# Storing each 128-row output tile by two 64-row transfers instead of one with an outer dimension of two

## The chip, the core and the metric

The kernel runs on one core of a Trainium2 chip. The metric is the time in microseconds (us) that one execution takes on the device, as the median of several runs. The engines are PE (TensorE, matrix products; PEld is its loading of weights), DVE (VectorE), ACT (ScalarE), POOL (GpSimd) and SP (SyncE). In this kernel SP issues every transfer between HBM and on-chip memory, one after the other; 16 DMA engines move the bytes.

## What is computed

A linear attention with a decaying state, over 4 batches, 8 heads, 768 tokens and head size 48, followed by a feed-forward layer whose activation is the square of a relu:

```python
for t in range(S):                       # state: [B, H, D, D]
    cur = einsum('bhd,bhe->bhde', u * k[t], v[t])
    y[t] = einsum('bhd,bhde->bhe', r[t], state + cur)
    state = w[t][..., None] * state + einsum('bhd,bhe->bhde', k[t], v[t])
x = y as [3072 tokens, 384]
out = square(maximum(x @ w_in, 0)) @ w_out        # w_in 384x2048, w_out 2048x384
```

Inputs and output are float32; the matrix products run in bfloat16.

## The kernel before, in words

The 3072 tokens are cut into 12 steps of 256 tokens, three steps for each batch. Within a step a partition holds two neighbouring tokens, an even and an odd one (`j` = 0 or 1), so that a 256-token block of `r`, `k`, `v` or `w` is one load of 384 KB into a tile of 128 partitions (`load_step`, L93). Four buffers of each input are there.

Attention of a step goes roughly so: `ww_` (POOL, L177) multiplies neighbouring decays, `lw_` (ACT, L181) takes the logarithm, `cum_` (PE, L217 to L220) sums it, `exp_` (ACT, L225 and L227) takes the exponential, `rd_` (DVE, L234) scales `r` and `k`. The result is transposed to `rkT`: by PE (L245) and a copy (L254) in the first four steps, by a transposing transfer from SP (`dtr_`, L257) in the other eight. `p_` (PE, L270) and `pm_` (DVE, L276) make the scores inside a block; `su_`, `ts_` and `sn_` (PE L290, DVE L299 and L301, POOL L305) carry the state on; `y_` and `yb_` (PE, L315) sum up the output. ACT casts `v` (`v_`, L185) for this, and POOL makes the terms of the current token (`ku_`, `qp_`, `vq_`, L197, L202 and L210). `y` is cast (L357) and transposed to `xT`, by PE in the first four steps and by a transposing transfer (`dyt_`, L373) in the others.

The feed-forward layer of a step then has 48 matmuls into the wide layer (`m1_`, L386), relu and square on ACT or DVE (L393, L395, L401, L403), and 32 matmuls back (`m2_`, L410), 16 for each of two tiles of 128 tokens (`c` = 0 or 1). `os_` (ACT, L415) copies such a tile from the accumulator to `o_sb`, 128 partitions by 384 float32, and `store` (L419) writes it out. There are 24 of these tiles, and four buffers for them.

In `o_sb`, partitions 0 to 63 hold the even tokens of the tile and partitions 64 to 127 the odd ones, while in the output even and odd rows alternate. The one transfer of `store` therefore has a three-dimensional target: 2 (even, odd) by 64 rows by 384 numbers, with the dimension of two outermost.

The order of all instructions is fixed when the kernel is built. A planner (`make_order`) knows for every operation (`op`) its engine, an assumed cost, a rank and what it depends on; for a transfer it also knows how long SP takes to issue it and how long the transfer is taken to occupy the DMA engines. It plays the schedule through and writes each engine's instructions in the order that comes out. On the chip each engine then works through its own list in that order and waits where an operand isn't there yet. So a wait holds up everything behind it on its engine, and a changed cost in the planner can change the order on every engine. The transfers use eight completion semaphores in turn, so each also waits until the one eight before it has landed.

Of the kernel before, what the change touches and what calls it, by code (L numbers as in the profile page):

```python
# [18 lines left out]
def kernel(  # L19
# [13 lines left out]
    nc = tc.nc  # L33
    PSUM = bass.MemoryType.PSUM

    B, H, S, D = r.shape
    C = 128
    Q = 64
# [101 lines left out]
    for c in range(2):  # L140
        rows = slice(c * Q, (c + 1) * Q)
# [21 lines left out]
    for c in range(2):  # L163
        rows = slice(c * Q, (c + 1) * Q)
# [7 lines left out]
    tiles = {}  # L172
# [243 lines left out]

    def store(s, c):
        t0 = s * T + c * C
        nc.sync.dma_start(out=out[t0:t0 + C, :].rearrange("(p j) d -> j p d", j=2),  # L419
                          in_=tiles.pop(("o", s, c))[:])  # L420

    def warm_(n):
        ps = ps_m2.tile([C, 512], FP32, name="m2")
# [9 lines left out]
    def op(eng, us, rank, fn, args, deps, take=(), give=None, dma=None):  # L433
        key = (fn.__name__,) + args
        plan[key] = (eng, us, rank, fn, args, deps, take, give, dma)

    def on(name, s, *rest):
        return [(name, s) + rest] if s >= 0 else []

    def by_dma(s):  # L440
        return s >= DMA_FROM
# [58 lines left out]
    for s in range(NS):  # L500
        at = AHEAD + s * 200
        xt = ("dyt_", s) if by_dma(s) else ("xt_", s)
        for g in range(8):
            deps = [xt] + [("cast", "i", g // 2, j) for j in range(KT)]
            if s >= 3:
                deps.append(("m2_", s - 3, 1, 3))
            op("P", .66, at + g, m1_, (s, g), deps, take=("m1",) if g % 2 else ("m1", "rl"))
            op(dict(A=.60, V=.68), None, at, rl_, (s, g), [("m1_", s, g)], give="m1")
            if g % 2:
                op(dict(A=1.05, V=.75), None, at, sq_, (s, g // 2), [("rl_", s, g - 1), ("rl_", s, g)],  # L510
                   give="rl")
        for c in range(2):
            for q in range(4):
                deps = [("sq_", s, q)]
                deps += [("cast", "o", q, j) for j in range(4)]
                if q:
                    deps.append(("m2_", s, c, q - 1))
                op("P", .65, at + AFTER + c * 4 + q, m2_, (s, c, q), deps,
                   take=() if q else ("m2",))
            op("A", .50, at - 5000, os_, (s, c), [("m2_", s, c, 3)] + on("store", s - 2, c), give="m2")  # L520
            op("S", .36, -1, store, (s, c), [("os_", s, c)], dma=(8, .54, 1.0))

    seq = [(0, x) for x in "wrukv"] + [(1, x) for x in "wrkv"] + [(g, "i") for g in range(4)]
    seq += [(2, x) for x in "wrkv"] + [(g, "o") for g in range(4)]
# [6 lines left out]
    for n, x in seq:  # L531
# [12 lines left out]
        dma = {"i": (24, 2.05, .9), "o": (32, 2.1, .9), "u": (8, .6, .9)}.get(x, (64, 1.73, .9))  # L544
# [147 lines left out]
```

## Time and profile before

| what | value |
|---|---|
| median of three runs | 230.69 us (230.67 to 230.79) |
| the profiled execution | 231.1 us |
| its span in the profile | 229.3 us |
| PE busy | 195.4 us, 85% of the span |
| DVE, ACT, POOL busy | 133.3, 109.0, 109.9 us |
| granted TensorE clock, mean | 0.967 |
| DMA traffic | 36.23 MB, mean 158 GB/s |
| stores of output tiles | 24, of 192 KB each, 0.52 us to issue (median) |

The profile is of one execution; all times "at" some point are us from the start of its span. The span leaves out 1.8 us that the device's own time of the same execution has (231.1 less 229.3). The views used below are the engines' busy time in stretches of time, which ends with the granted clock (1.00 is full speed), the mean busy share of the 16 DMA engines and the GB/s that they moved; the chain of work that ended last, which shows for each moment what the end of the run was waiting for; the instructions in order of time; and the list of who waited for whom. A sequencer's issue of a transfer is written SPq.

### The profile page before, as it was taken

Reading aid. Unit: us, or ns where it says so; the run is one execution under the profiler, and the core shown is the slowest. Engines: PE = TensorE matmul, PEld = TensorE weight load, DVE = VectorE, ACT = ScalarE, POOL = GpSimd, SP = SyncE. Lnnn points to the kernel's source line nnn. Section 1 sums busy time; section 2 is a strip of 40 time slices with the busy share of each in tenths; the row PEclk is TensorE's granted clock in tenths of the full one; section 3 lists DMA queues with packets and bytes.
Section 4 is the critical chain, followed back from the end, with each engine's and each line's share of the span. In section 5 each row is a group of like instructions: output and inputs, shape, how many; then the busy total and the mean of one; then the engine's idle time right before and its main releaser. Section 6 shows DMA issues by size and latency. Waiting matters only on the chain.

```text
span 229.3 us, 6128 instructions
## 1 busy us (share of the span) xinstructions
PE 195.4 (85%) x2637; PEld 130.3 (57%) x2637; DVE 133.3 (58%) x191; ACT 109.0 (48%) x177; POOL 109.9 (48%) x108
## 2 busy tenths in 40 slices
PE   7779999999989598897599994969498899999840
PEld 2335776667657354565366572747275577777520
DVE  4676897868759337283197754846376546445300
ACT  3418968876742466283573653460561332222200
POOL 6399595499983855931947733563720000000000
PEclk9999999999999979999799999999799999999995
DMA  7999999996697689946969659689948216111111
GB/s 170 236 300 377 262 304 362 223 273 174 176 121 209 164 81 238 150 125 168 204 162 219 152 155 138 172 139 177 118 81 104 51 33 65 38 39 38 37 50 38
DMA packets 80218, 36.23 MB, mean 158 GB/s; under 512 B 73408, under 2 KB 78656, under 8 KB 80192
## 3 DMA queue, kind: packets, MB, share of 16 engines
q1 hardware_dynamic: 80192, 35.86, 72.2%
q8 instruction: 20, 0.33, 0.6%
q14 instruction: 6, 0.05, 0.1%
HBM read 25.36 MB, written 4.72 MB: 131 GB/s over the span
## 4 chain that ended last, share of the span: by engine, by line
DMA 36%; PE 33%; SPq 9%; POOL 7%; ACT 4%; issue 4%; DVE 2%; POOLq 0%
PE m L410 14%; PE m L386 14%; DMA v_raw<-in_v_dram 10%; DMA w_raw<-in_w_dram 8%; SPq L93 6%; DMA w_st<-in_moe_w_in_dram 5%; DMA w_st<-in_moe_w_out_dram 4%; DMA k_raw<-in_k_dram 3%; DMA rkT<-rdec_buf 3%; DMA xT<-y_sb 3%; PE att L315 3%; POOL vq L210 2%; POOL ww L177 2%; POOL r_raw L189 1%; SPq L103 1%
## 5 line engine op out<-in xcount | busy, mean ns | idle before, releaser
L386 PE MATMUL m<-xT,wi_sb 128*128 128x256 bf16 x576 | 79.0, 278 | 4.1 <-ACT rl L393 2.6
L410 PE MATMUL m<-wo_sb,gt 128*128 128x384 bf16 x384 | 77.4, 331 | 5.4 <-ACT o_sb L415 5.0
L386 PEld LDWEIGHTS <-wi_sb 128*128 128x128 bf16 x576 | 55.6, 100 | 20.7 <-issue 5.4
L395 DVE TENSOR_SCALAR rl<-m 128x512 f16<-128x512 f32 x50 | 34.3, 690 | 34.7 <-PE m L386 34.7
L410 PEld LDWEIGHTS <-gt 128*128 128x128 bf16 x384 | 35.9, 98 | 25.9 <-issue 8.3
L393 ACT ACTIVATE rl<-m 128x512 f16<-128x512 f32 x46 | 27.1, 594 | 37.8 <-PE m L386 37.5
L276 DVE TENSOR_TENSOR pmT<-att,mask 128x1024 bf16<-128x1024 f32 x24 | 28.6, 1219 | 9.2 <-PE att L270 8.2
L401 ACT ACTIVATE gt<-rl 128x1024 bf16<-128x1024 f16 x24 | 25.3, 1056 | 1.3 <-DVE rl L395 0.7
L197 POOL TENSOR_TENSOR ku<-k_raw,u_bc 128x768 f32<-128x768 f32 x12 | 22.9, 1910 | 5.1 <-DMA k_raw<-in_k_dram 5.1
L210 POOL TENSOR_TENSOR vq<-v_raw,q 128x768 bf16<-128x768 f32 x12 | 17.9, 1491 | 14.0 <-DMA v_raw<-in_v_dram 4.5
L177 POOL TENSOR_TENSOR ww<-w_raw 128x384 f32<-128x384 f32 x11 | 11.0, 1000 | 25.1 <-DMA w_raw<-in_w_dram 25.1
L202 POOL TENSOR_TENSOR ku<-ku,r_raw 128x768 f32<-128x768 f32 x12 | 21.7, 1810 | 0.7
L185 ACT CAST v_bf<-v_raw 128x768 bf16<-128x768 f32 x12 | 10.0, 831 | 24.9 <-DMA v_raw<-in_v_dram 24.9
L415 ACT ACTIVATE o_sb<-m 128x384 f32<-128x384 f32 x24 | 11.7, 487 | 19.0 <-PE m L410 18.7
L403 DVE TENSOR_TENSOR gt<-rl 128x1024 bf16<-128x1024 f16 x24 | 18.1, 752 | 3.1 <-ACT rl L393 1.6
L425 PE MATMUL m<-warm 128*128 128x512 bf16 x61 | 18.0, 425 | 1.2 <-DVE half_ones L145 1.2
L193 POOL TENSOR_TENSOR k_raw<-k_raw,w_raw 128x384 f32<-128x384 f32 x11 | 11.7, 1062 | 8.6 <-DMA k_raw<-in_k_dram 8.1
L270 PE MATMUL att<-rkT 64*64 64x128 bf16 x384 | 8.9, 222 | 6.5 <-DMA rkT<-rdec_buf 6.4
L206 DVE TENSOR_REDUCE q<-ku 128x16 f32<-128x768 f32 x12 | 11.3, 944 | 5.1 <-POOL ku L202 5.1
L305 POOL TENSOR_TENSOR S<-t_state,a_c 128x192 bf16<-128x192 f32 x20 | 11.4, 571 | 6.0 <-DVE t_state L301 5.8
L301 DVE TENSOR_TENSOR t_state<-S,att 128x192 f32<-128x192 bf16 x16 | 5.6, 351 | 14.7 <-POOL S L305 11.7
L181 ACT ACTIVATE lw_buf<-ww 128x384 bf16<-128x384 f32 x12 | 6.2, 517 | 15.0 <-POOL ww L177 11.8
(64 smaller groups left out, 177.8 us busy)
## 6 DMA issues: line engine op xcount, KB each, us to landing
w_raw<-in_w_dram SPq DMA_DIRECT2D x12, 384.0 KB
r_raw<-in_r_dram SPq DMA_DIRECT2D x12, 384.0 KB
k_raw<-in_k_dram SPq DMA_DIRECT2D x12, 384.0 KB
v_raw<-in_v_dram SPq DMA_DIRECT2D x12, 384.0 KB
out_dram<-o_sb SPq DMA_DIRECT2D x24, 192.0 KB
w_st<-in_moe_w_in_dram SPq DMA_DIRECT2D x4, 768.0 KB
w_st<-in_moe_w_out_dram SPq DMA_DIRECT2D x4, 768.0 KB
rkT<-rdec_buf SPq DMA_TRANSPOSE x16
```

Of the source, the lines that this page charges most:

```text
L177: mul(ww[:], raw["w", s][:, :, 0, :], raw["w", s][:, :, 1, :])
L197: nc.gpsimd.tensor_mul(ku[:], raw["k", s][:, :, 1:3, :], u_bc[:, :, None, :].to_broadcast([C, H, 2, D]))
L202: nc.gpsimd.tensor_mul(ku[:], ku[:], raw["r", s][:, :, 0:2, :])
L210: nc.gpsimd.tensor_mul(vq[:].rearrange("p j h d -> p h j d"), raw["v", s][:], tiles.pop(("q", s))[:, :, :, None].to_broadcast([C, H, 2, D]))
L276: nc.vector.tensor_mul(tiles["pmT", s][:, f].rearrange("p a j t -> p a (j t)"), tiles.pop(("p", s, f))[:].rearrange("p e (a x) -> p (e a) ...
L386: nc.tensor.matmul(ps1[:, j, :], wi_sb[:, kk, n * 128:(n + 1) * 128], tiles["xT", s][:, :, kk, :], start=(kk == 0), stop=(kk == KT - 1))
L393: nc.scalar.activation(rl, m1[:], AF.Relu, scale=RS)
L395: nc.vector.tensor_scalar(out=rl, in0=m1[:], scalar1=RS, scalar2=0.0, op0=ALU.mult, op1=ALU.max)
L401: nc.scalar.activation(gt, rl[:], AF.Square)
L403: nc.vector.tensor_mul(gt, rl[:], rl[:])
L410: nc.tensor.matmul(tiles["m2"][:], gt[:, n, c * C:(c + 1) * C], wo_sb[:, n, :], start=(n == 0), stop=(n == NT - 1))
L425: nc.tensor.matmul(ps[:], warm[:, 0:C], warm[:], start=True, stop=True)
```

## The change

Each tile is stored by two transfers of 64 rows: the even tokens from partitions 0 to 63 and the odd tokens from partitions 64 to 127. Both sides of each are 64 rows by 384 numbers. The planner's figures for a store go with it: SP's issue from 0.36 to 0.9 us for the pair, and the time on the DMA engines from 0.54 to 0.6 us.

```diff
     def store(s, c):
         t0 = s * T + c * C
-        nc.sync.dma_start(out=out[t0:t0 + C, :].rearrange("(p j) d -> j p d", j=2),
-                          in_=tiles.pop(("o", s, c))[:])
+        o_sb = tiles.pop(("o", s, c))
+        rows = out[t0:t0 + C, :].rearrange("(p j) d -> j p d", j=2)
+        for j in range(2):
+            nc.sync.dma_start(out=rows[j], in_=o_sb[j * Q:(j + 1) * Q, :])
...
-            op("S", .36, -1, store, (s, c), [("os_", s, c)], dma=(8, .54, 1.0))
+            op("S", .9, -1, store, (s, c), [("os_", s, c)], dma=(8, .6, 1.0))
```

Because the planner's figures change, the order of later instructions changes too, on every engine. In the built program SP issues 129 transfers instead of 105; the lists of the engines agree up to the first steps and then differ in places: `rl` and `gt` pieces move between ACT and DVE (two instructions fewer on DVE, one more on ACT), and on SP one `k_raw` load near the end stands ahead of a transpose and a store that it stood behind.

## The prediction

> **What bounds the kernel now.** I read the busy time by stretches first. PE is the engine with the most work, so the question is where it stands idle:
>
> ```profile
> 72.00:180.00 108.00, 89.09 (x1330) 60.10 (x1327) 60.68 (x78) 52.11 (x83) 56.48 (x48) 0.95 0.83 151
> 180.00:217.00 37.00, 36.84 (x345) 26.58 (x344) 19.59 (x28) 11.88 (x21) 0.00 (x0) 1.00 0.20 41
> ```
>
> The columns are the stretch, its length, busy us of PE, PEld, DVE, ACT and POOL, granted clock, DMA share and GB/s. From 180 to 217 us PE has no idle time to give back. From 72 to 180 us it is idle for 108.0 - 89.1 = 18.9 us. The clock of 0.95 there is three dips: stretches of 3.4 us from 81.0, 111.7 and 162.9 show a clock of 0.50, each after a PE gap of 2 to 4 us. Half speed for 3 x 3.4 us loses 5.1 us. So 24.0 us stand in this stretch, and then there is the end, 217 to 229 us.
>
> Next the chain that ended last, for what those gaps wait on:
>
> ```profile
> 96.92 11.01 DMA w_raw<-in_w_dram
> ...
> 127.68 7.59 DMA w_raw<-in_w_dram
> ...
> 143.54 7.51 DMA v_raw<-in_v_dram
> ...
> 153.31 7.91 DMA v_raw<-in_v_dram
> ...
> 171.58 7.06 DMA rkT<-rdec_buf
> ```
>
> The columns are start, us, and what. Each of these begins just behind a store in SP's order, as the instructions of SP in order of time show:
>
> ```profile
> 95.65 1.18 SPq L419 DMA_DIRECT2D out_dram<-o_sb  x2
> 96.92 2.47 SPq L93 DMA_DIRECT2D w_raw<-in_w_dram  x1
> 99.48 3.77 SPq L93 DMA_DIRECT2D r_raw<-in_r_dram  x1
> ```
>
> The first `w_raw` of the run, issued at 0.74 with no store ahead, was in use at 4.58, after 3.8 us. Behind one store it takes 7.6, behind two 11.0. What the DMA engines do meanwhile is in stretches of one us:
>
> ```profile
> 102.00:103.00 1.00, 1.00 (x22) 0.52 (x20) 1.00 (x1) 0.41 (x2) 0.00 (x0) 1.00 0.13 50
> 103.00:104.00 1.00, 1.00 (x10) 0.73 (x8) 1.00 (x2) 0.87 (x3) 0.00 (x0) 1.00 0.15 54
> ...
> 221.00:222.00 1.00, 0.00 (x0) 0.00 (x0) 0.00 (x0) 0.00 (x0) 0.00 (x0) 1.00 0.13 49
> ...
> 227.00:228.00 1.00, 0.00 (x0) 0.00 (x0) 0.00 (x0) 0.00 (x0) 0.00 (x0) 0.50 0.13 49
> 228.00:229.00 1.00, 0.00 (x0) 0.00 (x0) 0.00 (x0) 0.00 (x0) 0.00 (x0) 0.50 0.00 0
> ```
>
> From 221 us on only stores are left, and the DMA share stands at 0.13 = 2/16. **A store runs on two of the 16 DMA engines**, at 49 to 50 GB/s: its 196.6 kB take 196.6/50 = 3.9 us. The same 0.13 between 102 and 104, with loads issued and POOL waiting 7.05 us for `w_raw`, says that 14 engines have nothing to do while two finish stores; a load has a share on every engine and is not there before the two are done. At the end,
>
> ```profile
> SPq L687 <- DMA out_dram<-o_sb: 7.0, 1, 7.0
> ```
>
> SP waits 7.0 us for the last store, behind which comes only the 1.0 us to the end of the span. The two last stores are issued 3.34 us apart and need 3.9 each, so the last also queues behind the one before.
>
> **The change, part by part.**
>
> *Width of a store.* Each half has 64 rows outermost on both sides. No transfer of 64 rows is in the trace, so the number of its engines is bounded: two, as now, from the store's own row, and 16 from the loads, whose 128-row tiles brought the DMA share to 1.06 and 305 GB/s between 3 and 40 us. I take 16, since the dimension of two is what the store has and no load has. The pair then occupies each engine for 3.9 x 2/16 = 0.5 us. With eight engines it would be 1.0.
>
> The Trainium skill's "DMA: Bandwidth & Descriptors", section "Rules for kernel authors", speaks against this change: two transfers to disjoint partition halves serialize, since both spray over all 16 engines anyway, and one 128-partition transfer is better. By that rule nothing is gained and 24 more issues are paid, up to 245.3 us. The 0.13 above contradicts its premise for this store. Another row of that table says that an outermost dimension below 16 confines the whole transfer to so many engines; by it 64 rows would get 16, which no run here has shown yet.
>
> *The end.* Today the last copy ends at 220.70, SP issues at 220.73, the last packet goes by 228.0, and the wait ends at 228.3. With the change: two issues take 1.18 us (the row at 95.65), to 221.91. The first packets of the store issued at 203.61 to 204.12 show at the latest at 205.2 (before, the DMA share is 0.00 in a quarter of a us), so 1.1 us; the packets take 0.5; from the last packet to the end of the wait 0.3, as now. That gives 223.8 instead of 228.3: **-4.5**. With two engines still, +0.6.
>
> *The middle.* What each chain row has above 3.9 us is the store's: 7.1, 3.7, 3.6, 4.0 and 3.2 us. The PE gaps that end on them, directly or over POOL, ACT and DVE, are 3.7 us at 107.6 (over `ww`, `lw` and `t_state`), 3.1 at 140.5 (over `rkT`), 1.1 at 150.8 (over `v_bf`), 3.0 at 160.4 (ACT stands in `v_bf` for 5.97 us, and `o_sb` is behind it) and 1.7 at 177.0: 12.6 us. Each is smaller than its excess, so each could close. Two of the dips follow them, 2 x 1.7 = 3.4 us: 16.0 together. I take four fifths, 12.8, since with the load in time the next operand is late by something, which the trace can't show. In 72 to 96 us the remaining gaps of 4.9 us and the dip's 1.7 go over `v_raw` (72.43, 6.73 us on the chain), whose buffers and SP position were set by earlier waits; I take a third, 2.3. Sum **-15.1**; bounds 0 and -24.0.
>
> *SP's issues.* 24 more at about 0.6 us (1.18 for two) are 14.6 us of SP, and everything behind a store, loads and transposes, is issued 0.6 later. I cost it at nothing beyond the end: a load's issue now takes up to 3.77 us (`r_raw` at 99.48) where 0.42 is the least, and that backlog goes with the long stores. If the cover is missing, each store on the chain costs 0.6: five places, 3.0 us. A pair also takes two of the eight semaphores, so the transfer eight places back, now seven to ten us old, must land a place earlier; the lateness of those is just what shrinks.
>
> *Order.* The moved `rl` and `gt` pieces cost 594 or 690 ns and 1056 or 752 ns by engine; two or three of them are under 1 us either way, and ACT and DVE are 48% and 58% busy. I take 0, with 2 us either way for waits that a new order may make.
>
> Sum, against the profiled execution: 231.1 - 4.5 - 15.1 = 211.5. It lies 0.4 above the median of the runs, so **211.1 us**.
>
> **The rivals.**
>
> *All gaps close.* 231.1 - 4.5 - 24.0 - 0.4 = 202.2 us. For it: the stretch before 72 us, where loads are ahead, has PE busy 24.3 of 25 us. Against: SP's list is strict, and eight steps need three transposes of 1.2 us issue each beside the loads and now four half-stores.
>
> *Mostly the end.* The next operand is late by nearly as much (SP's order and POOL's chain of `ww`, `ku`, `vq` become the bound), and the middle gives a third of 24 or less: 231.1 - 4.5 - 8.0 - 0.4 = 218.2, up to 226.2 with nothing from the middle. For it: chain rows of 7.00 us such as `xT` at 88.97, which waits behind three loads and no store.
>
> *Not wider, and slower.* The halves stay on two engines or fewer between them (each half was one engine's share). Then 3.9 us stay, and the issues are extra: 0.6 at the end and 0.6 on each of seven chain places from 56 us on, 4.9 us, 235.6; at most 14.6, 245.3. It decides where 3.9 - 7.8/k is under 0.6, which is k, the engines of the pair, at 2. Against it: two engines come with an outermost two.
>
> **How the numbers follow.** The forecast, 206 to 217 us: 0.52. All gaps, below 206: 0.17. Mostly the end, 217 to 230.2: 0.24, of that 0.18 below 222. Slower: 0.06. Within 0.2% of 230.69, about what a measurement of this kernel tells from none: 0.01. Faster is 0.52 + 0.17 + 0.24 = 0.93. The range of 203 to 222 leaves out some 0.06 below and 0.13 above.
>
> **What would show it.** Right: while only stores are left, the DMA share is near 1 for half a us and then 0, and SP's last wait is near 2 us; chain rows of `w_raw` and `v_raw` behind stores fall to about 4 us; issues of loads over 2.5 us become rare; the clock keeps 1.00 from 72 to 180. Wrong: a share of 0.13 or 0.06 behind a pair (width), rows of 7 us with the share high (a queue of loads, not stores), or PE gaps that end on POOL or SP's order with the loads landed.

## The result and the profile after

| | before | after |
|---|---|---|
| median | 230.74 us | 200.84 us (200.29 to 201.25) |
| ratio after/before | | 0.8697, interval 0.8666 to 0.8727 |
| profiled execution, its span | 231.1, 229.3 us | 200.29, 198.5 us |
| PE busy | 195.4 us, 85% | 188.4 us, 95% |
| mean granted clock | 0.967 | 1.0 |

The change saves 30 us, 13%, half as much again as the 19.6 us that were forecast (230.7 to 211.1), and the time lies under the range of 203 to 222. Here and below, a median is of all runs, while a ratio compares only the fast runs, those within 1.5% of the fastest of their kernel.

The busy time of the changed kernel in the stretch that the prediction is about (columns as before: PE, PEld, DVE, ACT, POOL, clock, DMA share, GB/s):

```profile
47.00:72.00 25.00, 25.00 (x387) 17.38 (x385) 19.96 (x27) 16.57 (x27) 23.83 (x22) 1.00 1.03 228
72.00:180.00 108.00, 107.81 (x1577) 75.60 (x1569) 72.32 (x93) 60.93 (x96) 52.04 (x45) 1.00 0.81 152
```

PE is idle for 0.2 us of 108 where it was idle for 18.9, and the clock holds 1.00. (Six of PE's 61 warming matmuls have no record in this profile; a second profile of the same kernel has all 61, and 189.2 us of PE.) SP's instructions in order of time, at a place like the one shown of before (two transfers of a tile, then the loads of a step):

```profile
99.45 1.18 SPq L422 DMA_DIRECT2D out_dram<-o_sb  x2
100.73 0.54 SPq L93 DMA_DIRECT2D w_raw<-in_w_dram  x1
101.37 0.62 SPq L93 DMA_DIRECT2D r_raw<-in_r_dram  x1
102.04 1.06 SPq L93 DMA_DIRECT2D k_raw<-in_k_dram  x1
103.20 1.28 SPq L93 DMA_DIRECT2D v_raw<-in_v_dram  x1
```

The pair costs SP 1.18 us, and the four loads behind it are issued in 3.5 us; before, `w_raw` and `r_raw` alone took 2.47 and 3.77. After 47 us, eight issues of loads took over 2.5 us before, and none does now. After 60 us the chain that ended last holds only these two transfers:

```profile
116.92 4.27 DMA k_raw<-in_k_dram
134.07 4.64 DMA v_raw<-in_v_dram
```

They take 4.3 and 4.6 us, where seven rows of 6.7 to 11.0 us stood. The end, in stretches of one us, and SP's last wait:

```profile
194.00:195.00 1.00, 0.25 (x2) 0.00 (x0) 0.00 (x0) 0.49 (x1) 0.00 (x0) 1.00 0.00 0
195.00:196.00 1.00, 0.00 (x0) 0.00 (x0) 0.00 (x0) 0.00 (x0) 0.00 (x0) 1.00 0.05 12
196.00:197.00 1.00, 0.00 (x0) 0.00 (x0) 0.00 (x0) 0.00 (x0) 0.00 (x0) 1.00 0.75 175
197.00:198.00 1.00, 0.00 (x0) 0.00 (x0) 0.00 (x0) 0.00 (x0) 0.00 (x0) 1.00 0.07 17
```
```profile
SPq L689 <- DMA out_dram<-o_sb: 1.5, 1, 1.5
```

Where only stores are left, the share is 0.75 for one us instead of 0.13 for seven, and SP waits 1.5 us instead of 7.0. A quarter of a us reaches a share of 0.91, which is 14.6 of the 16 engines: the half-tiles are not held to two engines.

**Where the 30.8 us of the span come from.** Behind PE's last matmul the span had 9.1 us (220.2 to 229.3) and has 4.2 (194.3 to 198.5): 4.9. The PE gaps from 72 to 180 give 18.7, the three clock dips there 5.1, the stretch from 47 to 72 (24.26 to 25.00 us busy) 0.7. That is 29.4; the remaining 1.4 lie outside these stretches and were not followed further.

### The profile page after: what moved, and what is told of

Its sections match the earlier page's. It is cut to its first block, busy times and chain, and to the rows that moved or that the text cites. A ratio compares the mean times of both kernels' runs of the same rounds, so it can differ in the third digit from the quotient of the medians.

```text
span 198.5 us, 6153 instructions
## 1 busy us (share of the span) xinstructions
PE 188.4 (95%) x2631; PEld 128.0 (64%) x2637; DVE 133.4 (67%) x189; ACT 111.2 (56%) x179; POOL 108.5 (55%) x108
## 4 chain that ended last, share of the span: by engine, by line
PE 65%; DMA 15%; SPq 7%; issue 5%; POOL 4%; ACT 2%; DVE 1%; POOLq 0%; ACTq 0%
PE m L410 27%; PE m L386 24%; PE att L315 6%; DMA w_raw<-in_w_dram 6%; DMA w_st<-in_moe_w_in_dram 5%; SPq L93 5%; PE att L270 2%; DMA v_raw<-in_v_dram 2%; DMA k_raw<-in_k_dram 2%; PE att L290 1%; SPq L103 1%; ACT o_sb L415 1%; POOL ku L202 1%; POOL ku L197 1%; PE att L219 1%
## 5 line engine op out<-in xcount | busy, mean ns | idle before, releaser
L386 PE MATMUL m<-xT,wi_sb 128*128 128x256 bf16 x576 | 76.7, 273 | 0.2 <-DVE rl L395 0.2
L410 PE MATMUL m<-wo_sb,gt 128*128 128x384 bf16 x384 | 75.8, 327 | 0.8 <-ACT o_sb L415 0.8
L386 PEld LDWEIGHTS <-wi_sb 128*128 128x128 bf16 x576 | 54.5, 98 | 15.3 <-issue 1.8
L393 ACT ACTIVATE rl<-m 128x512 f16<-128x512 f32 x47 | 27.9, 596 | 34.9 <-PE m L386 34.5
L401 ACT ACTIVATE gt<-rl 128x1024 bf16<-128x1024 f16 x25 | 26.4, 1057 | 5.5 <-DVE rl L395 5.0
L403 DVE TENSOR_TENSOR gt<-rl 128x1024 bf16<-128x1024 f16 x23 | 18.8, 819 | 2.3 <-ACT rl L393 0.6
L427 PE MATMUL m<-warm 128*128 128x512 bf16 x55 | 15.9, 414 | 1.3 <-DVE half_ones L145 1.2
L234 DVE TENSOR_TENSOR rdec_buf<-r_raw,att 128x768 bf16<-128x768 f32 x12 | 11.4, 950 | 3.0 <-ACT att L227 2.0
L189 POOL TENSOR_TENSOR r_raw<-r_raw,w_raw 128x384 f32<-128x384 f32 x11 | 11.6, 1051 | 0.5 <-DMA r_raw<-in_r_dram 0.5
L234 DVE TENSOR_TENSOR rdec_buf<-k_raw,att 128x768 bf16<-128x768 f32 x12 | 11.3, 946 | 0.0
```

The lines of the kernel that those rows point to most:

```text
L234: nc.vector.tensor_mul(rdec[:, i, :, :, 0:D], x.rearrange("p h j d -> p j h d"), cs[:, i, 0:DM].rearrange("p (h d) -> p h d", h=H)[:, None ...
L386: nc.tensor.matmul(ps1[:, j, :], wi_sb[:, kk, n * 128:(n + 1) * 128], tiles["xT", s][:, :, kk, :], start=(kk == 0), stop=(kk == KT - 1))
L393: nc.scalar.activation(rl, m1[:], AF.Relu, scale=RS)
L401: nc.scalar.activation(gt, rl[:], AF.Square)
L403: nc.vector.tensor_mul(gt, rl[:], rl[:])
L410: nc.tensor.matmul(tiles["m2"][:], gt[:, n, c * C:(c + 1) * C], wo_sb[:, n, :], start=(n == 0), stop=(n == NT - 1))
```

## The experiments

The theory: a store with the dimension of two outermost runs on two engines, and everything that shares these engines is late; PE pays for that lateness. Rivals: the new order pays a part; shorter transfers, not more engines, make the difference; SP's further issues cost something that the widening hides. One more rival needs no kernel of its own: that the long stores kept the four buffers of `o_sb` from being used again. In the profile before, all waits for a landed store come to 0.2 us, the end aside, so it is not that. Ratios are to the kernel before on the same chip.

**Two transfers, old planner figures.**

```diff
-op("S", .9, -1, store, ..., dma=(8, .6, 1.0))
+op("S", .36, -1, store, ..., dma=(8, .54, 1.0))
```

> Two transfers of 64 rows, but the planner keeps the old figures (0.36 and 0.54 us), so that the order on PE, DVE, ACT and POOL is that of the kernel before. If width is the whole cause: 200 to 202 us, PE gaps from 72 to 180 us near 0, as in the changed kernel. If the new order brings a part of the 30 us: clearly slower than 201, by that part; 205 or more would give the order a seventh.

200.04 us, ratio 0.863 (0.859 to 0.867). The same stretch:

```profile
72.00:180.00 108.00, 108.00 (x1583) 76.17 (x1580) 73.20 (x96) 59.57 (x94) 52.87 (x45) 1.00 0.82 153
```

PE has no gap at all in this stretch, in the order of the kernel before. The order is not the cause.

**One transfer, new planner figures.** The kernel before with only the planner's line of the change.

> One transfer with the outer dimension of two, but the planner's new figures (0.9 and 0.6 us). If width is the cause: 229 to 233 us, DMA share 0.13 where only stores are left. If the order brings the gain: near 201.

232.39 us, ratio 1.000 (0.996 to 1.004): the order alone changes nothing that can be seen.

**The order once more, on one chip.** The changed kernel and the first of these two again.

> The changed kernel once more, beside the two others of this call on one chip: 200 to 201.5 us.

> Two transfers of 64 rows in the order of the kernel before. If the planner's new figures cost something: 0.5 to 1.5 us below the changed kernel of this call. If what was seen was the chip: within 0.3 us of it.

200.00 us (0.8687, 0.8641 to 0.8733) and 200.17 us (0.8663, 0.8632 to 0.8693). The 0.8 us that lay between them on different chips are gone. The medians differ by 0.2 us, while the runs of the changed kernel alone reach from 199.7 to 202.4, so no effect of the order is seen.

**Four transfers a tile, of 62 and of 2 rows.**

```diff
 for j in range(2):
-    nc.sync.dma_start(out=rows[j], in_=o_sb[j * Q:(j + 1) * Q, :])
+    for lo, hi in ((0, 62), (62, 64)):
+        nc.sync.dma_start(out=rows[j][lo:hi], in_=o_sb[j * Q + lo:j * Q + hi, :])
```

> Each half is stored by a transfer of 62 rows and one of 2 rows, four transfers a tile. 62 has no divisor from 3 to 16. The Trainium skill's page on DMA (how many engines a transfer uses) makes 62 rows run on two engines: DMA share 0.13 again, and the time of the kernel before plus the issues. If it was the splitting into shorter transfers that helped, and not the number of engines: near 201 us plus up to 3 us of issues. If width is the cause and 62 rows get two engines: 230 to 240 us.

236.67 us, ratio 1.021 (1.015 to 1.026), and where only stores are left:

```profile
230.00:231.00 1.00, 0.00 (x0) 0.00 (x0) 0.00 (x0) 0.00 (x0) 0.00 (x0) 0.50 0.13 51
```

62 rows are on two engines again, and the gain is gone. Four transfers of 32 rows a tile, below, have as many issues and take 204.26 us. So not the shortness of the transfers helps but their width: between these two kernels lie 32 us. The rule drawn on is in the Trainium skill's "DMA: Bandwidth & Descriptors", section "Why a DMA increments its semaphore by 16 and not by 1": the number of engines is the largest up to 16 that divides the slowest dimension of both sides (the slowest that is not of size one). For 62 that is 2. The shares here, 0.13 for 2 and for 62, up to 0.91 for 64, agree.

**Every other store narrow.**

```diff
+if c == 0:
+    nc.sync.dma_start(out=rows, in_=o_sb[:])
+    return
 for j in range(2):
```

> The first tile of each step is stored by one transfer with the outer dimension of two, the second by two of 64 rows; planner figures of the changed kernel. Two engines then carry 3.9 us of narrow store a step instead of 7.9. If each store makes the loads behind it late by its own length and PE pays for it (the sum of the prediction): half of the middle's 24 us stays, 212 to 214 us. If PE waits only once the two engines have more work than a step is long, so that lateness adds up from step to step: nearly nothing stays, 201 to 204 us.

214.56 us, ratio 0.924 (0.918 to 0.930): by the two ratios 12.5 us above the changed kernel. Half of the narrow stores keep four tenths of the loss. The reading that PE waits only once two engines are overfull fell. The stretch and three rows of the chain:

```profile
72.00:180.00 108.00, 98.98 (x1484) 67.55 (x1483) 64.81 (x84) 57.71 (x89) 55.13 (x48) 0.97 0.86 154
```
```profile
83.50 6.63 DMA v_raw<-in_v_dram
93.89 7.44 DMA w_raw<-in_w_dram
...
159.81 6.89 DMA rkT<-rdec_buf
```

9.0 us of gaps and two clock dips stay. Rows of 7 us remain, those of 11 are gone. `w_raw` at 93.89 and `rkT` at 159.81 stand right behind a narrow store; the chain's two `k_raw` rows at 126.07 and 138.86, with no narrow store right ahead, take 4.24 and 4.02 us. But `v_raw` at 83.50, with 6.63, has none right ahead either.

**Only the last seven tiles wide.** The kernel before, with two transfers of 64 rows from the 18th tile on.

> The order and the single narrow transfer of the kernel before, but the last seven tiles are stored by two transfers of 64 rows. With width as the cause the end and the middle add up: only the end gains, 4.9 us as in the changed kernel, so 225 to 226.5 us, and the PE gaps from 72 to 180 us stay as before. If the end's gain came with the middle (a queue that had grown until then), less than 3 us.

226.28 us, ratio 0.984 (0.975 to 0.994). The middle:

```profile
72.00:180.00 108.00, 89.65 (x1317) 59.76 (x1316) 59.01 (x76) 51.08 (x80) 56.32 (x48) 0.92 0.81 150
```

It is as before, and PE's last matmul ends at 220.2 us as before. Behind it stand 4.1 us instead of 9.1: the end gains alone, 5.0 us in the profile and 4.6 between the medians (the interval of the ratio reaches from 1.4 to 5.8). End and middle add up.

**Narrow stores behind the loads.**

```diff
-op("S", .36, -1, store, ...)
+op("S", .36, 1, store, ...)
```

> The kernel before with its narrow stores, but the planner ranks a store behind the loads that are ready, so that some stores go behind two or more loads on SP and several come together near the end of the loads. The two engines carry as many bytes. If what counts is the delay of the loads and transposes that stand right behind a store: some of the middle's 24 us goes, 220 to 227 us. If the bytes on two engines count, wherever they stand: 229 to 233 us.

233.25 us, ratio 1.005 (1.001 to 1.010). This other place in SP's list brings nothing. In the profile, PE's gaps are 17.6 us from 72 to 180, 1.3 less than before, and 4.6 us from 47 to 72, where 0.7 stood: they moved. That fits the reading that the bytes on two engines count, wherever they stand, and does not prove it.

A count in the kernel before fits too. Of the 115 stretches of one us from 47 to 162, one has a DMA share under 0.12 (it has 0.10), as it would be if two engines had work nearly all the time; in the changed kernel eleven have. The share does not tell which engines work, so this is an argument. If every load needs those two, the loads come at their pace: `w_raw` was issued at 96.9, 113.6, 127.7 and 144.1 us, every 15.7 us, while PE needs 14.2 a step ((194.3 - 23.6)/12 in the changed kernel, from its first `m1_` matmul). Now they come at 89.3, 100.7, 113.4 and 125.7, every 12.1. But with every other store narrow the pace is 13.1, and with the narrow stores behind the loads 13.7 (98.0 to 139.2); both are under 14.2, and PE still waits. So pace alone doesn't settle it, and single late loads count too. How the two share the loss stays open.

**More issues, all on 16 engines.** Four transfers of 32 rows and eight of 16 rows a tile, in place of two of 64.

```diff
-    nc.sync.dma_start(out=rows[j], in_=o_sb[j * Q:(j + 1) * Q, :])
+    for h in range(2):                                   # or 4, with 16 rows each
+        nc.sync.dma_start(out=rows[j][h * 32:(h + 1) * 32],
+                          in_=o_sb[j * Q + h * 32:j * Q + (h + 1) * 32, :])
```

> The changed kernel, but four transfers of 32 rows a tile, still on 16 engines: two more issues of about 0.6 us on SP before whatever stands behind a store. If SP's issues are covered, as the prediction costs them: only the end pays, about 1.2 us, so 201.5 to 202.5. If loads behind a store are already just in time, each store on the way costs 1.2 us: 205 us or more.

> The changed kernel, but eight transfers of 16 rows a tile, on 16 engines: six more issues than two transfers, about 3.6 us of SP at each store, as long as a narrow store occupied its two engines. The end pays 3.6 us. If the middle has room for delays on SP of that size: 204 to 206 us. If a delay of 3.6 us behind each store costs PE what the narrow stores cost it: 225 us or more. It is to show whether the middle closed so completely because there is room, or because nothing is late any more.

204.26 us (0.885, 0.880 to 0.890) and 235.16 us (1.019, 1.012 to 1.026). In the first, SP's issue of one tile and the stretch from 72 to 180 us:

```profile
101.86 1.93 SPq L423 DMA_DIRECT2D out_dram<-o_sb  x4
```
```profile
72.00:180.00 108.00, 104.94 (x1556) 73.30 (x1554) 70.47 (x92) 59.16 (x95) 52.35 (x46) 1.00 0.78 151
```

In the second, SP's instructions and the same stretch:

```profile
95.72 8.38 SPq L423 DMA_DIRECT2D out_dram<-o_sb  x16
104.20 0.40 SPq L93 DMA_DIRECT2D w_raw<-in_w_dram  x1
...
114.42 3.83 SPq L423 DMA_DIRECT2D out_dram<-o_sb  x8
```
```profile
72.00:180.00 108.00, 90.20 (x1313) 59.59 (x1310) 58.97 (x76) 53.41 (x84) 54.63 (x48) 0.94 0.73 152
```

Two tiles keep SP for 8.38 us, and `w_raw` waits behind them. PE loses 17.8 us in the stretch and the clock dips, just as with the narrow stores, although each piece is wide: in stretches of 0.05 us near the end the share goes up to 0.61, about ten engines, and back to 0.00 between the pieces. From 227 to 231 us, where only stores are left, that averages to a share of 0.19 to 0.21 and 49 to 52 GB/s, no more than the narrow stores moved. The limit is now the issue of a piece every 0.46 us. The eight semaphores are not it: SP waits 0.9 us in this whole run for landings of earlier transfers, its last wait aside.

A tile costs SP 3.83 us here, 1.93 with quarters, 1.18 with halves. 0.75 us more a tile already cost 3.4 us: PE is idle for 3.1 us of the stretch, and the end is hardly longer (3.9 us behind the last copy, with halves 3.7). So the middle closed because nothing was late any more, and not because there is room: the room is smaller than 0.75 us a tile.

**One transfer on all engines, order mended by the matmuls.** Output rows in natural order, `m1_` reading `xT` with even and odd tokens alternating.

```diff
-tiles["xT", s][:, :, kk, :],
+tiles["xT", s][:, :, kk, :].rearrange("p c (j t) -> p c t j", j=2),
...
-out=out[t0:t0 + C, :].rearrange("(p j) d -> j p d", j=2)
+out=out[t0:t0 + C, :]
```

> One transfer of 128 rows in natural order, on all engines, 24 issues instead of 48: the tokens are put in order by the matmuls of the first layer, which read the columns of xT as 64 pairs with a stride of 64 (even and odd alternating) instead of 128 in a row; planner figures of the kernel before. If width is what counts: as the changed kernel or up to 0.6 us faster at the end, 199.5 to 201, unless the strided operand makes the 576 matmuls of L386 slower than their 273 ns.

274.48 us, ratio 1.189. The group of these matmuls (busy us, mean ns; matmuls overlap, so the busy time is what counts):

```profile
L386 PE MATMUL m<-xT,wi_sb 128*128 128x256 bf16 x576 | 153.5, 405 | 0.0
```

79.0 us have become 153.5: the strided operand nearly doubles them.

**One transfer on all engines, order mended by relu.** The same store, with the alternation where relu reads the accumulator:

```diff
+rl = rl.rearrange("p a (c t j) -> p (a c) t j", c=2, j=2)
+m1 = m1[:].rearrange("p a (c j t) -> p (a c) t j", c=2, j=2)
```

> One transfer of 128 rows in natural order on all engines; the tokens are put in order where relu reads the accumulator (L393 and L395 read even and odd tokens alternately, with a stride of 64 numbers), so that no matmul reads a strided operand; planner figures of the kernel before. SP has one issue of about 0.36 us a tile instead of two of 0.53. If the relus keep their 594 and 690 ns: 0.7 us less at the end than the changed kernel, so 199.3 to 200.3 us. If strided reads slow them to over 1 us: ACT and DVE, with 96 of them, become late, 205 us or more.

> One transfer of 128 rows in natural order, ordered by relu's reads, with the planner's new figures (0.9 and 0.6 us). If the issue saved at the end and nothing else makes that version faster: 0.7 us below the changed kernel of this call. If it was the old order: no faster than the changed kernel.

199.13 us (0.861, 0.858 to 0.865) and, with the new figures beside the changed kernel's 200.00 us on one chip, 199.04 us (0.861, 0.858 to 0.864). The relus of the first of these:

```profile
L397 DVE TENSOR_SCALAR rl<-m 128x512 f16<-128x512 f32 x50 | 34.4, 690 | 32.3 <-PE m L386 32.3
L395 ACT ACTIVATE rl<-m 128x512 f16<-128x512 f32 x46 | 27.3, 596 | 38.1 <-PE m L386 37.8
```

They keep their 690 and 596 ns. This version is faster than both kernels, by 1.0 us than the changed one. The store has one issue of 0.41 us (median) a tile instead of two, and the end shows the gain: 2.9 us behind the last copy, where the changed kernel has 3.8 on the same chip.

## Why the prediction was wrong

- **Two engines, and 16 for the halves: right.** The share of 0.13 was the width, shown by the changed kernel (up to 0.91) and by the 62 rows (0.13 again). Against the rule of the Trainium skill's "DMA: Bandwidth & Descriptors", section "Rules for kernel authors", that two transfers to disjoint partition halves aren't worth it, the measurement decides: with an outermost two, the one transfer was not on all engines, and splitting it saved 30 us. The same table's row on using all 16 engines held.
- **The end, -4.5: 4.9 measured** (5.0 in the profile where the last seven tiles alone were wide). The wait is 1.5 us where I worked out 1.9. I had the first packets at 205.2 at the latest, but a share of 0.16 from 204.75 to 205.00 shows them before 205.0.
- **The middle, -15.1: 23.8 measured.** This is the step that failed. I found 24.0 us there, rightly, and then discounted it: a fifth of the 16.0 us tied to chain rows (3.2), two thirds of the 6.6 from 72 to 96 us (4.3; a third of 6.6 is 2.2, not 2.3), and the last 1.4 us of gaps, which got no term and no reason. For the fifth I wrote "since with the load in time the next operand is late by something, which the trace can't show", and no row stood behind it. With wide stores PE is busy 107.8 and 108.0 of 108 us in either order: nothing else was late. I had also read each of the five chain rows as standing just behind a store; `v_raw` at 153.31 has a `k_raw` load between. Gaps without a store right ahead closed like the others, so the narrow stores held up more than the next transfer in the list. By which path, the runs leave open.
- **What had no term.** The stretch from 47 to 72 us gave 0.7 us and the rest of the run 1.4. With 8.7 in the middle and 0.4 at the end that is the 11.2 us by which the span fell further than the 19.6 forecast.
- **SP's issues at nothing beyond the end: right for two transfers, for a reason that is thinner than I gave.** The issue backlog did go, and the version with one issue a tile gains its 1.0 us at the end, but 0.75 us more a tile costs 3.4 us. (24 issues at 0.59 us, half of 1.18, are 14.2 us, not 14.6.) As an argument against the rival "all gaps close", SP's strict list was a true limit, not yet reached.
- **Order at 0 with 2 us either way: right**; 0.2 us between medians on one chip. One `rl` and one `gt` piece went from DVE to ACT, which makes two instructions more on ACT (177 to 179), not one.
- **The rivals.** "All gaps close", 202.2 us, is what happened, and I gave it 0.17; it missed 0.4 us at the end and what had no term. "Mostly the end" fell. "Not wider, and slower" is the 62-row kernel: 236.7 us, with two issues a tile more than the rival had at 235.6.

## What to carry to other kernels

Where a stretch holds only one kind of transfer and they follow each other without a pause, its DMA share times 16 is the number of engines it uses. With pauses it is less: the 16-row pieces average 0.20 and reach 0.61 while they move. A steady 0.13 on a 128-partition store was worth a change of its shape here, because loads behind such stores took 7.6 and 11.0 us instead of about 4. Where one cause stands ahead of most gaps and no row shows what would come next, take the whole of the gaps as the forecast and put the doubt into the range; in this case that would have given 202.2 us. Splitting a transfer has its price on the queue that issues it: past the point where it widens, each further piece delays all that stands behind it.

## What the runs showed of the hardware that was not expected

- A transfer's issue on SP does not grow with its rows: 0.42 us (median) for 16 or 32 rows by 384 numbers, 0.59 for 64, 0.36 to 0.41 for 128 in natural order, 0.52 for 2 by 64.
- A matmul whose moving operand alternates between two places 64 bf16 numbers apart takes about twice its time: 153.5 us against 79.0 for 576 of them. The same alternation in ACT's and DVE's reads of the float32 accumulator costs nothing (596 and 690 ns against 594 and 690).
